# Linear attention and two MLPs on one core: two more blocks of the first MLP done as a pair by seven products of halves, with the preparation's tiles and stores arranged anew

## The chip, the cores and the metric

The kernel runs on one core of a Trainium2 chip. The metric is the device time of one execution in microseconds (us). The engines named here are TensorE (PE: matmuls; its weight loads are listed as PEld), VectorE (DVE), ScalarE (ACT), GpSimd (POOL) and SyncE (SP), which issues most of the DMA transfers. A row with a q behind the engine's name (SPq, ACTq) is that engine's instruction queue at work, for example issuing a transfer.

## The reference

All data is float32 (the weights arrive as 64-bit floats, read as pairs of 32-bit words). Three stages follow each other:

```
kv  = einsum('bhsd,bhse->bhde', k, v)              # batch 8, heads 8, seq 576, dim 64
o   = einsum('bhsd,bhde->bhse', q, kv)
x   = o / sqrt(mean(o*o, -1) + 1e-6) * g_norm      # 4608 tokens x 512
h   = x @ w_in                                     # 512 -> 2048
g   = h if h >= 1, 0 if h <= -1, else (h + 1)**2 / 4
x   = g @ w_out                                    # 2048 -> 512
h   = x @ w_in2
out = (max(h, 0)**2) @ w_out2
```

## The kernel before

**Blocks.** The 4608 tokens are nine blocks of 512 (numbered 0 to 8). Blocks 0 to 7 are the first 512 positions of the eight batch entries; block 8 collects the 64 positions that are left of each. The first MLP (L = 1) takes block after block, each in 16 steps over the 2048 inner columns. In a step `h_stage` makes 12 matmuls into one bank, ScalarE and VectorE make the activation, `g_stage` splits the result into a high and a low part, and `out_stage`, LAG = 2 steps later, adds 12 matmuls to four accumulator banks. Every product of two float32 matrices is three matmuls of high and low parts (`mm3`), each of 128 x 128 weights and 512 columns.

**Attention** of block b + 1 runs beside the steps of block b, cut into stages (`kv_stage`, `t_stage`, `o_stage`, `r_stage`) that a table of hooks puts at half steps. Attention 7 so runs beside block 6, and none runs beside blocks 7 and 8. Block 8's input, `xrd`, is stored batch entry by batch entry and loaded again.

**The second MLP** (L = 2) works on pairs of blocks, (0,1), (2,3), (4,5), (6,7), and on block 8 alone at the end. For a pair, both of its matrix products are taken as 2 x 2 halves with seven products where eight would do (`PRODUCTS`). `in_phase` goes through four groups q of seven products of two inner tiles each, reads sums and differences of halves of x (`x2_jobs`) against prepared sums and differences of halves of the weights, and makes the activation of each bank; `out_phase` goes through seven products of eight inner tiles. Each phase has 28 weight tiles with 12 matmuls for each tile. `put_out` transposes the result on VectorE and stores it, during the next pair.

**The preparation** makes those weight tiles while the first MLP runs. It has 16 units, each for two tiles of 128 rows or columns of one weight matrix of L = 2: load two raw tiles (`prep_load`), narrow them from 64 to 32 bits (`prep_narrow`, lines 227 to 230), make four sums of 256 columns (`prep_sums`, lines 294 to 298), and split four tiles (`prep_split`, line 305), storing two of them whole (`wcd`, line 308) and seven halves (`wsd`, line 315). The stores are issued by SP, as soon as the code reaches them. All its tiles share three buffers (`w1_13` to `w1_15`) with the raw loads. Those buffers are free because the last TAIL = 6 of the 16 second weight tiles of L = 1 are stored and fetched again for each block from 1 on (`load_tail`, line 254), over RING = 3 buffers.

**Order.** A planner orders the instructions of each engine by priority and by its own reckoning of when they can run, so the order written in the code is a priority and not the order of execution. At run time each engine and each queue takes its instructions in the order that the planner left.

Lines 735 (split), 758 (differences of x), 812 to 852 (`in_phase`), 862 to 923 (`out_phase`), 877 and 880 (its sums) and 665 (store of a finished block of L = 1) are spoken of below.

Of the kernel before, what the change touches and what calls it, by code (L numbers as in the profile page):

```python
# [76 lines left out]
def linear_attention_rms_two_mlps(  # L77
# [36 lines left out]
    TAIL = 6  # L114
# [4 lines left out]
    EVERY = 7  # L119
# [12 lines left out]

    x1d = [dr.tile([P, KD, TB], F32, name=f"x1d{b}") for b in range(NB)]
    xrd = dr.tile([P, KD, B, REM], F32, name="xrd")
    wtd = [dr.tile([P, 2 * TB], F32, name=f"wtd{f}") for f in range(TAIL)]
# [99 lines left out]
    def split_w(L, f, which):  # L235

        phase = int(f >= AHEAD)
        w = narrow_w(L, f, which, phase)
        dst = wi if which == 0 else wo
        t = wp.tile([P, 2, TB], F32R, tag=f"w{which}_{f}", name=f"w{L}_{which}_{f}")  # L240
        split(t, w, "w", phase)
        dst[L, f] = t
        if which == 1 and f >= NF - TAIL:
            nc.sync.dma_start(wtd[f - (NF - TAIL)], t.rearrange("p a f -> p (a f)").bitcast(F32))

# [4 lines left out]
    def load_tail(b, f):  # L250

        i = f - (NF - TAIL)
        t = wp.tile([P, 2, TB], F32R, tag=f"w1_{NF - TAIL + i % RING}", name=f"wt{b}_{f}")
        nc.sync.dma_start(t.rearrange("p a f -> p (a f)").bitcast(F32), wtd[i])
        wo[1, f] = t


    prep_tags = itertools.cycle(range(NF - RING, NF))
# [6 lines left out]
    def prep_load(which, i):  # L265
        for f in (i, i + NH):
            t = prep_tile(f"raw2_{which}_{f}", [P, 2 * TB], I32)
# [10 lines left out]
    def prep_narrow(which, i, n):  # L278
        prep[which, i, n] = narrow_w(2, i + n * NH, which, 2)

    def halves(which, i):

        w0, w1 = prep[which, i, 0], prep[which, i, 1]
        lo, hi = slice(0, H2), slice(H2, TB)
        if which == 0:
            return w0[:, lo], w0[:, hi], w1[:, lo], w1[:, hi]
        return w0[:, lo], w1[:, lo], w0[:, hi], w1[:, hi]

    def prep_sums(which, i):
        a11, a12, a21, a22 = halves(which, i)  # L290
        t = d_tile(f"s12_{which}_{i}")
        u = d_tile(f"s34_{which}_{i}")
# [6 lines left out]
        prep[which, i, 2], prep[which, i, 3] = t, u  # L299

    def prep_split(which, i, n):
        src = prep.pop((which, i, n))
        t = prep_tile(f"s2_{which}_{i}_{n}", [P, 2, TB], F32R)
        copy(engine2("s_hi"), t[:, 0, :], src)
        engine2("s_lo").tensor_tensor(t[:, 1, :], src, t[:, 0, :].bitcast(F32), ALU.subtract)
        t = t.bitcast(F32)
        if n < 2:
            nc.sync.dma_start(wcd[which, i + n * NH], t)
        made = {
            0: ((1, 2), (None, 4), (5, 6), (7, 3)),  # L310
            1: ((1, None), (2, 4), (5, 6), (7, 3)),
        }[which][n]
        for h, p in enumerate(made):
            if p:
                nc.sync.dma_start(
                    wsd[which, i // 2, p][:, i % 2], t[:, :, h * H2 : (h + 1) * H2]
                )
# [8 lines left out]
    og = {}  # L326

# [17 lines left out]
    def load_kv(b, hp):  # L345
        h0 = 2 * hp
        if b > 0:

            r = rests[hp % len(rests)]
# [56 lines left out]
    def kv_stage(b, *hps):  # L406
# [12 lines left out]
        for n, hp in enumerate(hps):  # L419
            for j in range(2):  # L420
# [8 lines left out]
                t = kvbd[hp % len(kvbd)]  # L429
# [72 lines left out]
    def o_stage(b, hp, half):  # L502
        work, parts = hl[b, hp]
        kv = kvbd[hp % len(kvbd)]
# [23 lines left out]
    def r_stage(b, hp):  # L528
# [19 lines left out]
        norm(t, y, o)  # L548
        nc.gpsimd.tensor_copy(xrem[b][:, hp, :], t[:, TB:])
        split(xs[1, b][hp], t[:, :TB], "x", b)  # L550
# [6 lines left out]
    def attention(b):  # L557
# [6 lines left out]
        def begin():  # L564
            new_x(1, b)
# [590 lines left out]
```

## Time and profile before

| | |
|---|---|
| Time, median of 3 runs | 1595.66 us (1595.51 to 1598.09) |
| Time of the profiled execution | 1596.07 us |
| Span of the profiled execution | 1594.3 us |
| PE busy | 1579.0 us (99%), 7531 matmuls |
| DVE busy | 942.4 us (59%) |
| ACT busy | 906.8 us (57%) |
| POOL busy | 111.0 us (7%) |
| Moved by DMA | 302.36 MB, mean 190 GB/s |

The span reaches from the first to the last instruction in the trace. Busy times are those of the whole span; the stages differ a lot, so the rows below are taken by stage. The end of a matmul is modelled in the profile, so that a busy PE is not PE at its peak.

### The profile page before, as it was taken

Reading aid. Unit: us, or ns where it says so; the run is one execution under the profiler, and the core shown is the slowest. Engines: PE = TensorE matmul, PEld = TensorE weight load, DVE = VectorE, ACT = ScalarE, POOL = GpSimd, SP = SyncE. Lnnn points to the kernel's source line nnn. Section 1 sums busy time; section 2 is a strip of 40 time slices with the busy share of each in tenths; the row PEclk is TensorE's granted clock in tenths of the full one; section 3 lists DMA queues with packets and bytes.
Section 4 is the critical chain, followed back from the end, with each engine's and each line's share of the span. In section 5 each row is a group of like instructions: output and inputs, shape, how many; then the busy total and the mean of one; then the engine's idle time right before and its main releaser. Section 6 shows DMA issues by size and latency. Waiting matters only on the chain.

```text
span 1594.3 us, 21133 instructions
## 1 busy us (share of the span) xinstructions
PE 1579.0 (99%) x7531; PEld 1292.5 (81%) x7533; DVE 942.4 (59%) x1558; ACT 906.8 (57%) x1649; POOL 111.0 (7%) x106
## 2 busy tenths in 40 slices
PE   9999999999999999999999999999999999999998
PEld 5788888788888888888888888888888888878886
DVE  6976756557666575643244348754974496457522
ACT  5976666666666676744344556446635663665321
POOL 0000000000000000000000121012101300330000
PEclk9999999999999999999999999999999999999999
DMA  9926656675776757522140457596768666865683
GB/s 283 281 93 164 209 163 212 178 238 185 221 218 191 235 170 226 191 71 93 53 145 27 171 190 247 189 234 208 240 193 243 218 217 202 237 220 186 189 249 104
DMA packets 306969, 302.36 MB, mean 190 GB/s; under 512 B 195504, under 2 KB 248752, under 8 KB 306864
## 3 DMA queue, kind: packets, MB, share of 16 engines
q1 hardware_dynamic: 304880, 300.22, 61.2%
q8 instruction: 60, 0.98, 0.2%
q10 hardware_dynamic: 1984, 0.79, 0.2%
q14 instruction: 45, 0.37, 0.1%
HBM read 231.74 MB, written 69.21 MB: 189 GB/s over the span
## 4 chain that ended last, share of the span: by engine, by line
PE 70%; issue 15%; DVE 9%; ACT 2%; DMA 2%; POOL 1%; SPq 0%; DVEq 0%; POOLq 0%; ACTq 0%
PE acc L197 27%; PE ph L197 26%; PE ph L790 10%; PE po L790 4%; DVE t L735 3%; DVE x L735 2%; PE po L197 1%; PE pkv L418 1%; PE pr L540 1%; POOL t L851 1%; DVE g L880 1%; DVE xr L758 1%; DMA q<-in_q_dram 0%; POOL g L852 0%; DMA wsd<-s 0%
## 5 line engine op out<-in xcount | busy, mean ns | idle before, releaser
L197 PE MATMUL ph<-x,w 128*128 128x512 f32 x1728 | 419.0, 391 | 2.4 <-ACT w L176 1.5
L197 PEld LDWEIGHTS ph<-x,w 128*128 128x128 f32 x1728 | 321.8, 188 | 70.1 <-ACT w L176 2.3
L790 PE MATMUL po<-t,ws 128*128 128x512 f32 x1344 | 307.3, 390 | 1.8 <-DVE t L735 1.8
L790 PE MATMUL ph<-x,ws 128*128 128x512 f32 x1344 | 306.5, 389 | 0.6 <-DVE e L835 0.6
L790 PEld LDWEIGHTS po<-t,ws 128*128 128x128 f32 x1344 | 251.4, 188 | 57.0 <-DVE t L735 5.0
L790 PEld LDWEIGHTS ph<-x,ws 128*128 128x128 f32 x1344 | 252.0, 188 | 54.1 <-DVE e L835 1.9
L197 PE MATMUL acc<-gs,w 128*128 128x512 f32 x1152 | 280.6, 392 | 0.0
L197 PEld LDWEIGHTS acc<-gs,w 128*128 128x128 f32 x1152 | 214.4, 188 | 44.6 <-DVE u L614 0.3
L612 ACT ACTIVATE u<-ph,halfb 128x512 f32<-128x512 f32 x144 | 99.2, 689 | 176.8 <-PE ph L197 176.6
L614 DVE SCALAR_TENSOR_TENSOR u<-u,ph 128x512 f32<-128x512 f32 x144 | 98.4, 683 | 166.3 <-ACT u L183 165.9
L735 DVE TENSOR_TENSOR t<-g,t 128x512 fp32r<-128x512 f32 x192 | 134.7, 708 | 74.2 <-ACT t L176 71.8
L176 ACT CAST t<-g 128x512 fp32r<-128x512 f32 x192 | 116.4, 621 | 71.4 <-DVE t L735 50.8
L189 DVE TENSOR_TENSOR gs<-u,gs 128x512 fp32r<-128x512 f32 x160 | 110.4, 690 | 63.2 <-ACT gs L176 62.0
L176 ACT CAST gs<-u 128x512 fp32r<-128x512 f32 x160 | 99.4, 621 | 75.2 <-DVE u L614 58.0
L197 PE MATMUL acc<-gs,wt 128*128 128x512 f32 x576 | 139.4, 391 | 0.0
L197 PEld LDWEIGHTS acc<-gs,wt 128*128 128x128 f32 x576 | 106.8, 188 | 21.6
L843 DVE TENSOR_TENSOR h<-ph,e 128x512 f32<-128x512 f32 x96 | 66.1, 691 | 55.9 <-PE ph L790 50.2
L844 ACT ACTIVATE h<-h 128x512 f32<-128x512 f32 x96 | 60.5, 630 | 60.0 <-DVE h L843 56.0
L183 ACT ACTIVATE u<-u 128x512 f32<-128x512 f32 x144 | 91.1, 632 | 2.2
L851 POOL TENSOR_TENSOR t<-g 128x512 f32<-128x512 f32 x32 | 43.1, 1347 | 633.7 <-ACT g L845 353.2
L845 ACT ACTIVATE g<-h 128x512 f32<-128x512 f32 x128 | 80.9, 632 | 3.6
L835 DVE TENSOR_TENSOR e<-ph,e 128x512 f32<-128x512 f32 x64 | 43.4, 688 | 44.3 <-PE ph L790 43.2
(116 smaller groups left out, 1415.0 us busy)
## 6 DMA issues: line engine op xcount, KB each, us to landing
ws<-wsd SPq DMA_DIRECT2D x224, 512.0 KB, 3.5
wsd<-s SPq DMA_DIRECT2D x112, 256.0 KB, 3.8
wt<-wtd SPq DMA_DIRECT2D x48, 512.0 KB, 4.4
raw<-in_moe_w_in_dram SPq DMA_DIRECT2D x32, 512.0 KB, 5.9
raw<-in_moe_w_out_dram SPq DMA_DIRECT2D x32, 512.0 KB, 5.7
wcd<-s SPq DMA_DIRECT2D x32, 512.0 KB, 3.6
ws<-wcd SPq DMA_DIRECT2D x32, 512.0 KB, 4.3
x1d<-ev SPq DMA_DIRECT2D x36, 256.0 KB, 3.0
```

The source lines that it names most:

```text
L176: return e.copy(dst, src)
L183: e.activation(dst, src, AF.Square)
L189: lo = engine(op + "_lo", phase).tensor_tensor(t[:, 1, :], src, t[:, 0, :].bitcast(F32), ALU.subtract)
L197: nc.tensor.matmul(dst, wt(a), xt(c), start=first and n == 0, stop=last and n == 2)
L612: nc.scalar.activation(u, ps, AF.Relu, bias=halfb, scale=0.5)
L614: nc.vector.scalar_tensor_tensor(u, u, 1.0, ps, op0=ALU.min, op1=ALU.max)
L735: engine2(op + "_lo").tensor_tensor(t[:, 1, :], src, t[:, 0, :].bitcast(F32), ALU.subtract)
L790: nc.tensor.matmul(ps, wt(a), xt(c), start=first and n == 0 and i == 0, stop=last and n == len(lhs) - 1 and i == 2, skip_group_check=True,)
L843: nc.vector.tensor_tensor(h, bank, add, ALU.add)
L844: nc.scalar.activation(h, h, AF.Relu)
L845: nc.scalar.activation(g, h, AF.Square)
L851: engine2("t_sum").tensor_tensor(t1[k], b, a, ALU.subtract)
```

## The change

Blocks 7 and 8 leave the plain loop of the first MLP. They are taken as a pair (1, 7), third in a list of five pairs, by the same two phases that the pairs of the second MLP use, with the first MLP's activation and with all 16 differences of the activations (`t_sum`) on VectorE for that pair. Attention 7 stores its result (`xpd`, `xrd`) and the pair loads it through `x2_jobs`. The result of the pair is stored to `x1d` without a transpose.

For this the weights of L = 1 must be there as sums and differences of halves too. Each unit of the preparation goes on after its four tiles of L = 2: it adds the high and low parts of two tiles of L = 1 (`prep_join`), makes their four sums, and splits and stores two more tiles. `keep_first` stores those halves of the L = 1 tiles that are themselves used. Nine tail tiles are fetched for each block, where it was six. The raw tiles have two buffers of their own, the split tiles four. All weight tiles are laid out as [128, half, high or low, 256], and each matrix pair has one store `wsd[L, w, a]` of eight slots, from which both the halves and whole tiles are read; `wcd` and `wtd` go.

Stores of split tiles and of finished blocks no longer go out on SP at once: `owe` notes them with a delay of two half steps (one for finished blocks), and `pay`, called once in each half step, issues them on ScalarE's queue. The hooks are numbered by half steps; `o_stage` and `r_stage` come one half step later, the first x load of a next pair comes six products earlier.

```diff
-    TAIL = 6
+    TAIL = 9
...
+    PLAIN = B - 1
+    PAIRS = [(2, 0), (2, 2), (1, PLAIN), (2, 4), (2, 6)]
+    LAST_B = B - 1
...
     wsd = {
-        (w, a, p): dr.tile([P, 2, 2, H2], F32, name=f"wsd{w}_{a}_{p}")
+        (L, w, a): dr.tile([P, 8, 2, 2, H2], F32, name=f"wsd{L}_{w}_{a}")
+        for L in (1, 2)
         for w in range(2)
         for a in range(NQ)
-        for p in PRODUCTS
     }
-    wcd = {(w, f): dr.tile([P, 2, TB], F32, name=f"wcd{w}_{f}") for w in range(2) for f in range(NF)}
...
+    MADE = {
+        0: (1, 2, None, 4, 5, 6, 7, 3),
+        1: (1, None, 2, 4, 5, 6, 7, 3),
+    }
+    def keep_halves(L, which, i, n, t, now=False):
+        made = MADE[which][2 * n : 2 * n + 2]
+        hs = slice(0, 2)
+        if L == 1 and None in made and not (which == 1 and i + n * NH >= NF - TAIL):
+            hs = slice(1, 2) if made[0] is None else slice(0, 1)
+        dst = wsd[L, which, i // 2][:, 2 * n + hs.start : 2 * n + hs.stop, i % 2]
+        if now:
+            nc.sync.dma_start(dst, t[:, hs])
+        else:
+            owe(2, dst, t[:, hs])
+    owed = []
+    tick = [0]
+    def owe(wait, dst, src):
+        owed.append((tick[0] + wait, dst, src))
+    def pay(every=False):
+        for job in list(owed):
+            due, dst, src = job
+            if every or due <= tick[0]:
+                nc.scalar.dma_start(dst, src)
+                owed.remove(job)
+        tick[0] += 1
+    def split_halves(t, src, hi, lo):
+        src = src.rearrange("p (h f) -> p h f", h=2)
+        copy(hi, t[:, :, 0, :], src)
+        lo.tensor_tensor(t[:, :, 1, :], src, t[:, :, 0, :].bitcast(F32), ALU.subtract)
...
+    raw_tags = itertools.cycle((NF - TAIL + RING, NF - TAIL + RING + 1))
+    prep_tags = itertools.cycle(range(NF - TAIL + RING + 2, NF))
...
+    def prep_join(L, which, i):
+        for n in range(2):
+            f = i + n * NH
+            t = prep.get((L, which, i, n))
+            if t is not None:
+                d, w = t[:, :, 0, :], t
+            else:
+                w = (wi[L, f] if which == 0 else wo[L, f]).bitcast(F32)
+                d = d_tile(f"j_{which}_{f}").rearrange("p (h f) -> p h f", h=2)
+            nc.vector.tensor_tensor(d, w[:, :, 0, :], w[:, :, 1, :], ALU.add)
+            prep[L, which, i, n] = d
...
+    def prep_split(L, which, i, n):
+        src = prep.pop((L, which, i, n))
+        t = prep_tile(f"s{L}_{which}_{i}_{n}", [P, 2, 2, H2], F32R)
+        split_halves(t, src, engine2("s_hi"), engine2("s_lo"))
+        keep_halves(L, which, i, n, t.bitcast(F32))
+    def keep_first(which, f):
+        t = wi[1, f] if which == 0 else wo[1, f]
+        keep_halves(1, which, f % NH, f // NH, t.bitcast(F32), now=True)
...
+        xt = st.tile([P, TB], F32, tag="st", name=f"xt_{hp}")
+        nc.vector.scalar_tensor_tensor(t, t, -3.0, y, op0=ALU.add, op1=ALU.mult)
+        nc.vector.tensor_tensor(xt, o[:, :TB], t[:, :TB], ALU.mult)
+        nc.vector.tensor_tensor(xrem[b][:, hp, :], o[:, TB:], t[:, TB:], ALU.mult)
+        x_kept[hp] = xt
+    x_kept = {}
+    def keep_x(b, hp):
+        nc.sync.dma_start(xpd[:, hp, :], x_kept.pop(hp))
+        nc.sync.dma_start(xrd[:, hp, b, :], xrem[b][:, hp, :])
...
+                (s + 3, o_stage, b, hp, 0),
+                (s + 4, o_stage, b, hp, 1),
...
+            slots.append((s + 6, r_stage, b, hp))
+            if b == LAST_B:
+                slots.append((s + 8, keep_x, b, hp))
...
-            nc.sync.dma_start(x1d[b][:, c, :], t)
+            owe(1, x1d[b][:, c, :], t)
...
+    def x_source(n, b, ch, t):
+        L, b0 = PAIRS[n]
+        if L == 2:
+            return t, x1d[b0 + b][:, ch, :]
+        if b == 0:
+            return t, xpd[:, ch, :]
+        return t.rearrange("p (b s) -> p b s", b=B), xrd[:, ch, :, :]
...
-                        h = tmp.tile([P, TB], F32, f"h{n}_{p}_{k}")
-                        if p == 2:
-                            nc.scalar.activation(h, bank, AF.Relu)
-                        else:
+                        h = bank
+                        if p != 2:
+                            h = tmp.tile([P, TB], F32, f"h{n}_{p}_{k}")
                             add = e[i, {5: 7, 4: 1, 3: 6}[p]]
                             nc.vector.tensor_tensor(h, bank, add, ALU.add)
-                            nc.scalar.activation(h, h, AF.Relu)
-                        nc.scalar.activation(g, h, AF.Square)
+                        if PAIRS[n][0] == 1:
+                            nc.scalar.activation(g, h, AF.Relu, bias=halfb, scale=0.5)
+                            nc.scalar.activation(g, g, AF.Square)
+                            nc.vector.scalar_tensor_tensor(g, g, 1.0, h, op0=ALU.min, op1=ALU.max)
+                        else:
+                            u = tmp.tile([P, TB], F32, f"u{n}_{p}_{k}") if p == 2 else h
+                            nc.scalar.activation(u, h, AF.Relu)
+                            nc.scalar.activation(g, u, AF.Square)
                 yield
             for i in range(2):
                 k = 2 * q + i
                 a, b, d = g2[k][0][:, 0, :], g2[k][0][:, 1, :], g2[k][1][:, 1, :]
                 t1[k] = t1_ring.tile([P, TB], F32, f"t1_{n}_{k}")
-                engine2("t_sum").tensor_tensor(t1[k], b, a, ALU.subtract)
-                engine2("t_sum").tensor_tensor(b, d, b, ALU.subtract)
+                for dst, x, y in ((t1[k], b, a), (b, d, b)):
+                    e = nc.vector if PAIRS[n][0] == 1 else engine2("t_sum")
+                    e.tensor_tensor(dst, x, y, ALU.subtract)
...
+        if L == 1:
+            for m in range(2):
+                nc.sync.dma_start(x1d[b][:, 2 * hm + m, :], result[n](hm, m, hn))
+            return
...
+    kept = [(w, f) for f in range(NF) for w in range(2) if w == 0 or f < NF - TAIL]
+    for j, (w, f) in enumerate(kept):
+        hook(2 * (NF + 2) + 3 * j, keep_first, w, f)
...
     for j in range(2 * NH):
         which, i = j % 2, j // 2
-        s0 = NF + 2 + (7 * j * (7 * NF - 8)) // (7 * 2 * NH)
-        for d, half, f, a in (
-            (0, 0, prep_load, ()),
-            (1, 0, prep_narrow, (0,)),
-            (2, 0, prep_narrow, (1,)),
-            (3, 0, prep_sums, ()),
-            (3, 1, prep_split, (0,)),
-            (4, 0, prep_split, (1,)),
-            (4, 1, prep_split, (2,)),
-            (5, 0, prep_split, (3,)),
+        s0 = 2 * NF + 4 + (j * 164) // 16
+        for d, L, f, a in (
+            (-6, 2, prep_load, ()),
+            (2, 2, prep_narrow, (0,)),
+            (3, 2, prep_narrow, (1,)),
+            (4, 2, prep_sums, ()),
+            (4, 2, prep_split, (0,)),
+            (5, 2, prep_split, (1,)),
+            (6, 2, prep_split, (2,)),
+            (7, 2, prep_split, (3,)),
+            (7, 1, prep_load, ()),
+            (9, 1, prep_join, ()),
+            (10, 1, prep_sums, ()),
+            (10, 1, prep_split, (2,)),
+            (11, 1, prep_split, (3,)),
         ):
-            hook(0, s0 + d, half, f, which, i, *a)
-    last = (NB - 1) * NF
+            hook(s0 + d, f, L, which, i, *a)
...
+    last = 2 * (PLAIN - 1) * NF
     first_x = x2_jobs(0, Ring(*[(st, "st")] * 7))
     when = [0, 1, 2, 3, 4, 5, 6, 7, 5, 8, 9, 10, 11, 12, 13, 14]
     for t, f in zip(when, first_x):
-        hook(0, last + t, 1, f)
-    for i in range(7):
-        hook(0, last - 3 + i if i < 3 else last + i, 1, load_w2)
+        hook(last + 2 * t + 1, f)
+    for i, t in enumerate((7, 9, 11, 13, 15, 21, 23)):
+        hook(last + t, load_w2)
...
+            pay(True)
...
-        at = range(8, 8 + 2 * len(jobs), 2)
+        at = (2, *range(10, 8 + 2 * len(jobs), 2))
```

## Rows read from the trace of the kernel before

**Rows 1.** Windows: busy us by engine, PE's clock, DMA share, GB/s
```profile
45.00:141.00 96.00, 94.56 (x502) 74.24 (x501) 75.69 (x138) 74.57 (x147) 2.56 (x4) 1.00 0.58 177
141.00:237.80 96.80, 96.80 (x510) 80.04 (x509) 62.42 (x112) 64.51 (x127) 1.80 (x4) 1.00 0.63 187
...
335.70:432.70 97.00, 97.00 (x512) 80.87 (x511) 59.13 (x104) 62.82 (x123) 1.36 (x4) 1.00 0.70 214
...
717.10:804.10 87.00, 87.00 (x385) 72.03 (x384) 27.61 (x42) 34.76 (x56) 0.00 (x0) 1.00 0.22 73
...
1038.00:1115.00 77.00, 76.79 (x339) 63.29 (x338) 36.15 (x54) 42.98 (x72) 17.90 (x12) 1.00 0.77 220
1115.00:1192.00 77.00, 76.77 (x338) 62.84 (x337) 64.08 (x98) 42.69 (x75) 6.30 (x4) 1.00 0.67 218
```

**Rows 2.** Waits: engine, line, releaser: us in total, times, longest us
```profile
DVE u L614 <- ACT u L183: 165.9, 73, 4.3
...
PE po L790 <- DVE t L735: 1.8, 4, 1.1
```

**Rows 3.** Timeline of SP: stores of finished blocks (start us, us)
```profile
716.92 2.25 SPq L665 DMA_DIRECT2D x1d<-ev  x4
...
803.96 1.15 SPq L665 DMA_DIRECT2D x1d<-ev  x2
...
891.00 2.25 SPq L665 DMA_DIRECT2D x1d<-ev  x4
```

**Rows 4.** The chain that ended last: the same place in two pairs
```profile
1086.42 28.88 PE ph L790 x126
...
1240.07 28.87 PE ph L790 x126
```

**Rows 5.** Instruction groups: busy us, mean ns of one; idle before, releaser
```profile
L614 DVE SCALAR_TENSOR_TENSOR u<-u,ph 128x512 f32<-128x512 f32 x144 | 98.4, 683 | 166.3 <-ACT u L183 165.9
...
L843 DVE TENSOR_TENSOR h<-ph,e 128x512 f32<-128x512 f32 x96 | 66.1, 691 | 55.9 <-PE ph L790 50.2 <-ACT h L844 5.7
...
L230 DVE SCALAR_TENSOR_TENSOR d<-raw,d 128x512 int32<-128x512 int32 x64 | 43.7, 686 | 4.9 <-ACT raw L227 3.6
L835 DVE TENSOR_TENSOR e<-ph,e 128x512 f32<-128x512 f32 x64 | 43.4, 688 | 44.3 <-PE ph L790 43.2
...
L227 ACT ACTIVATE raw<-raw 128x512 f32<-128x512 f32 x64 | 42.7, 679 | 17.7 <-DMA raw<-in_moe_w_in_dram 9.7 <-DMA raw<-in_moe_w_out_dram 4.4 <-DMA wt<-wtd 3.6
...
L229 DVE TENSOR_SCALAR d<-raw 128x512 int32<-128x512 int32 x64 | 26.6, 419 | 19.8 <-DMA raw<-in_moe_w_in_dram 13.3 <-DMA raw<-in_moe_w_out_dram 6.4
...
L305 DVE TENSOR_TENSOR s<-s,s 128x512 fp32r<-128x512 f32 x32 | 21.9, 684 | 2.5 <-ACT s L176 2.2
...
L176 ACT CAST s<-s 128x512 fp32r<-128x512 f32 x32 | 19.9, 623 | 5.6 <-DVE s L297 3.4 <-DMA wsd<-s 2.2
...
L294 DVE TENSOR_TENSOR s<-d 128x256 f32<-128x256 f32 x8 | 3.4, 419 | 0.1
```

**Rows 6.** Windows: two stretches of the first block, same columns
```profile
65.00:75.00 10.00, 10.00 (x44) 7.79 (x43) 9.73 (x19) 9.94 (x21) 0.00 (x0) 1.00 1.01 307
95.00:105.00 10.00, 10.00 (x61) 8.07 (x60) 10.00 (x20) 9.90 (x20) 0.24 (x1) 1.00 0.69 249
```

**Rows 7.** Timelines of SP's and ACT's queues: issues (start us, us)
```profile
159.15 1.25 SPq L315 DMA_DIRECT2D wsd<-s  x2
...
0.76 0.74 ACTq L400 DMA_DIRECT2D kvr<-in_k_dram  x1
```

**Rows 8.** Waits of SP's queue: us in total, times, longest
```profile
SPq L308 <- DVE s L305: 51.7, 10, 19.7
```

**Rows 9.** The tile of the tail weights, its loads
```profile
DMA to landing us min/median/max: 3.1/4.4/10.1
```

**Rows 10.** Timeline of 1086 to 1115 us (start us, us)
```profile
1086.42 28.86 PE L790 MATMUL ph<-x,ws 128*128 128x512 f32 x126 [0.21 <-DVE e L835]
...
1099.70 0.69 DVE L877 TENSOR_TENSOR g<-g,t 128x512 f32<-128x512 f32 x1 [1.37 <-POOL t L851]
```

More of the change, by code (lines that the diff above doesn't have):

```diff
@@ L239, in split_w, with kept_whole @@
         dst = wi if which == 0 else wo
-        t = wp.tile([P, 2, TB], F32R, tag=f"w{which}_{f}", name=f"w{L}_{which}_{f}")
-        split(t, w, "w", phase)
+        t = wp.tile([P, 2, 2, H2], F32R, tag=f"w{which}_{f}", name=f"w{L}_{which}_{f}")
+        split_halves(t, w, engine("w_hi", phase), engine("w_lo", phase))
         dst[L, f] = t
         if which == 1 and f >= NF - TAIL:
-            nc.sync.dma_start(wtd[f - (NF - TAIL)], t.rearrange("p a f -> p (a f)").bitcast(F32))
+            keep_halves(L, which, f % NH, f // NH, t.bitcast(F32), now=True)
+    def kept_whole(L, which, f):
+        return wsd[L, which, f % NH // 2][:, f // NH * 2 : f // NH * 2 + 2, f % 2]
     def split_later(*a):
@@ L276, in prep_load, with prep_narrow, halves, prep_sums @@
             w_raw[2, f, which] = t.rearrange("p (f two) -> p f two", two=2)
[L278 to L284, printed above, removed]
-        if which == 0:
[L286 to L292, printed above, removed]
+    def prep_join(L, which, i):
+        for n in range(2):
+            f = i + n * NH
+            t = prep.get((L, which, i, n))
[6 more added lines that the diff above has]
+            prep[L, which, i, n] = d
+    def prep_narrow(L, which, i, n):
+        prep[L, which, i, n] = narrow_w(2, i + n * NH, which, 2)
+    def halves(L, which, i):
+        w0, w1 = prep[L, which, i, 0], prep[L, which, i, 1]
+        if L == 2:
+            w0, w1 = (w.rearrange("p (h f) -> p h f", h=2) for w in (w0, w1))
+        if which == 0:
+            return w0[:, 0, :], w0[:, 1, :], w1[:, 0, :], w1[:, 1, :]
+        return w0[:, 0, :], w1[:, 0, :], w0[:, 1, :], w1[:, 1, :]
+    def prep_sums(L, which, i):
+        a11, a12, a21, a22 = halves(L, which, i)
+        t = d_tile(f"s12_{L}_{which}_{i}")
+        u = d_tile(f"s34_{L}_{which}_{i}")
         s1, s2, s3, s4 = t[:, :H2], t[:, H2:], u[:, :H2], u[:, H2:]
@@ L555, in new_x, with begin, attention_first @@
         ]
-    def attention(b):
+    def begin(b):
+        if b < LAST_B:
+            new_x(1, b)
+        xrem[b] = ap2.tile([P, KD, REM], F32, tag="xrem", name=f"xrem_{b}")
+    def attention_first():
         slots = {}
@@ L719, in load_w2 @@
             return
-        whole = len(key) == 2
-        t = w_ring.tile([P, 2, TB] if whole else [P, 2, 2, H2], F32R, "ws" + "_".join(map(str, key)))
-        nc.sync.dma_start(t.bitcast(F32), (wcd if whole else wsd)[key])
+        name = "ws" + "_".join(map(str, key))
+        if len(key) == 4:
+            t = w_ring.tile([P, 2, 2, H2], F32R, name)
+            L, which, a, p = key
+            nc.sync.dma_start(t.bitcast(F32), wsd[L, which, a][:, MADE[which].index(p)])
+        else:
+            which, f = key
+            t = w_ring.tile([P, 2, 2, H2], F32R, name)
+            nc.sync.dma_start(t.bitcast(F32), kept_whole(2, which, f))
         w_loaded.append((key, t))
@@ L950, in put_out @@
                 nc.sync.dma_start(rows[a], src)
[L952 removed]
+    blocks = [(1, b) for b in range(PLAIN)]
     hooks = {}
[L955 to L994 removed]
@@ new lines, in hook @@
+    def hook(s, f, *a):
+        hooks.setdefault((s // 2, s % 2), []).append((f, a))
+    jobs = [(0, store_xrem, 0)]
+    for b in range(1, B):
+        jobs += attention(b, 2 * NF * (b - 1), 7, range(NP))
+    for job in sorted(jobs, key=lambda j: j[0]):
+        hook(*job)
+    for i in range(NF):
+        later = split_later if i < 2 else split_w
+        for w, ahead, at in ((0, 7, 6), (1, 6, 3)):
+            if i + ahead < NF:
+                hook(2 * i + w, load_w, 1, i + ahead, w)
+            if i + at < NF:
+                hook(2 * i + w, later, 1, i + at, w)
@@ L1052, in linear_attention_rms_two_mlps @@
     nc.gpsimd.memset(kvw, 0.0)
-    first = attention(0)
+    first = attention_first()
     for s, n in WARMS:
```

180 lines of the change are left out of this document (68 added, 112 removed).

## The prediction

> **What bounds the kernel now.** First the busy time by stage [rows 1]. TensorE is busy for the whole of every window after the start, at granted clock 1.00, which is its level of 2.4 GHz, and the number of matmuls in a window follows the length of the window: 385 records in the 87.00 us of a first-layer block beside which no attention runs, 339 and 338 in the two halves of a pair of the second layer. VectorE is busy for 28 to 79% of these windows, ScalarE for 40 to 78%. Then the waits: the longest that TensorE has against another engine in the pairs sums to 1.8 us in four times [rows 2]. Then the moments at which the blocks end. The stores of the evicted block follow each other by 803.96 - 716.92 = 87.04 and 891.00 - 803.96 = 87.04 us [rows 3]; a block is 16 steps of 12 + 12 matmuls, 384, so one takes 226.7 ns. A pair of the second layer has 672 matmuls (28 weight tiles of 12 in each half) and comes round after 1240.07 - 1086.42 = 153.65 us [rows 4], 228.6 ns each. So time goes by the count of matmuls, at one price, in stages with VectorE nearly idle and in stages with VectorE at 83%. The profiled run took 1596.07 us for a span of 1594.3, so 1.8 lie outside it; the median of the runs shown is 1595.66, 0.4 less. I sum against 1596.07 and take 0.4 off.
>
> **The change, part by part.**
>
> *The pair in place of blocks 7 and 8.* Two blocks of 87.04 us go: block 7's attention is already done during block 6, and stays there. One more round of the pair loop comes: 153.65 us, with its two transitions, since the period is taken from round to round. Net 174.08 - 153.65 = -20.4 us. By the count it is 96 matmuls at 226.7 ns, -21.8; the 1.3 us between are the pair's own small gaps. I take -20.4.
>
> *The activation inside the new pair.* Per bank of the first product stage it keeps the two ScalarE steps and adds one VectorE step that reads the sum a second time (32 in all; like line 614, 683 ns: 21.9 us), and it moves 16 differences from GpSimd to VectorE (684 ns by line 305: 10.9 us) [rows 5]. VectorE had 36.15 us of work in that half [rows 1]; it gets 36.15 + 21.9 + 10.9 = 69 of 77 us, 90%. The second half already runs with 64.08 of 77, and TensorE's longest wait there, the 1.8 us of [rows 2], is that stage's. Below: nothing. Above: the rival in order, below. I take 0.5 us. The following pair loses the 8 transposes of `put_out`, off the path: nothing.
>
> *The preparation.* A unit (there are 16) had on VectorE 2 x (419 + 686) + 4 x 419 + 4 x 684 ns = 6.6 us, on ScalarE 2 x 679 + 4 x 623 = 3.85 us [rows 5]. Now it also joins two first-layer tiles, makes their four sums, and splits two more tiles: + 2 x 684 + 4 x 419 + 2 x 684 = 4.4 us on VectorE (11.0), + 1.25 on ScalarE (5.1). The units were spread over 104 steps, 2.46 a block; now over 164 half steps, 3.12 a block. Block 3 (the window from 335.7 [rows 1]) then goes on VectorE from 59.1 to 59.1 - 16.3 + 34.5 = 77 us of 97, 80%, and on ScalarE from 62.8 to 62.8 - 9.5 + 15.9 = 69 us. The cover is shown by the first block, with 75.69 and 74.57 us of 96, 79 and 78%, and TensorE busy for 94.56 of them; and stretches of 10 us in which both engines stand at 9.7 to 10.0 have TensorE at 10.00 as well [rows 6]. LAG holds two steps between activation and second product, so short crowding is swallowed. I take 0.5 us for the seven blocks, bounds 0 and what the rivals give.
>
> *Stores from ScalarE's queue.* Six stores a unit and four of each block's result are issued from ScalarE: 6 x 3.12 + 4 = 23 a block. An issue of such a store takes SP 1.25/2 = 0.63 us, and one on ScalarE's own queue took 0.74 [rows 7]. So ScalarE gets 14 to 17 us more, 83 to 86 of 97. A store waiting at the head would hold the activations behind it, and the matmuls behind those; being due two half steps (6 us) after the split was issued, it should find its tile written. ScalarE would pass TensorE's 97 us only if an issue cost (97 - 69)/23 = 1.2 us. Below: nothing; above: nothing up to 1.2. I take nothing. SP loses the waits that it had at these stores (51.7 us in ten at line 308 alone [rows 8]), so the loads behind them (tails, raw tiles, q, k, v) leave earlier; as nothing on TensorE waits for them now, that gains nothing.
>
> *The rings of their own.* Raw tiles get two tiles and split tiles four, where both shared three; nine tail tiles a block are fetched over three buffers, not six. A tail load still leaves when the product three before it ends and is due two steps later, about 13 us; it lands after 4.4 us in the middle and 10.1 at most [rows 9]. Nothing, unless the DMA engines fill up.
>
> *What the DMA engines get.* A unit moved 2 raw tiles, 2 whole and 7 half stores, 3.9 MB; now 2 raw, 4 + 2 whole stores and 9/16 of a load, 4.5 MB: 9.7 to 14.0 MB a block. Three tails more are 1.6 MB. The kept first-layer tiles are 8.1 MB over 67 half steps, 3.9 MB a block in blocks 1 to 3. That is 9.8 MB a block more there, 5.9 after. The window at 717.1 moved 73 GB/s at a share of 0.22 [rows 1], 6.35 MB, so 1 MB costs 87 x 0.22 / 6.35 = 3.0 us of all sixteen. On 0.63 to 0.70 of a block (the windows from 141 and 335.7) come 0.30, making 0.93 to 1.0 in blocks 1 to 3, and 0.81 to 0.88 after. I take 1 us; the bounds are in the rivals. The Trainium skill, page "DMA: Bandwidth & Descriptors", section "Issuing engines are not separate DMA queues", says that transfers issued by several engines run on the same sixteen and interleave, so that a second issuer saves issue time alone. No row before shows stores from ScalarE's queue beside loads from SP's. By that rule the moved stores relieve the engines of nothing and the 1 us stands; were ScalarE's queue apart, it would be 0.
>
> *The rest.* First x loads of a pair go out at product 2, not 8, in a stage without a wait for them: nothing. Attention's o and r stages move one half step later; o's and r's matmuls waited for nothing that counts: nothing. The first pair's x tiles and attention 7 now share the seven `st` buffers in block 6; a load that waits there for a buffer holds SP, and could hold TensorE at `kv_stage` by about a landing, 4 us [rows 9]. I take nothing, bound 4.
>
> **Sum.** 1596.07 - 20.4 + 0.5 + 0.5 + 1 = 1577.7, as a median 1577.3; I say 1577.5.
>
> **The rivals.**
>
> *The DMA engines fill up (0.18).* For: 0.93 to 1.0 by the sum above, in blocks 1 to 3. Against: stores now go out in runs of 2 KB for 1 KB, and loads have 13 us and more of lead. Were the demand 5% over, the backlog would be 2.1 x 97 x 0.05 = 10 us, which TensorE would spend waiting for tails or k and v: about 1587; it begins to cost above 1.0. The case runs from 1581 to 1592. By the rule named above this case keeps its chance; without it the chance would be near nothing.
>
> *VectorE takes the new pair's steps in the written order (0.07, slower).* Place: the first half of the new pair. In the code each bank's third step follows its add at once. If VectorE stood still between them while ScalarE does two steps (1.32 us), a bank would cost 0.69 + 1.32 + 0.68 + 0.05 = 2.75 us, against 1.37 that TensorE takes for it. Four rounds of 6 such banks, 2 without the add (2.0 each), 4 adds and 4 differences are 104 us, with the 8.5 of transposes and preparation 112 for 77: +35, so about 1612. It decides from 20 us of such standing on. For it: VectorE stood 165.9 us in 73 times for just this pair of steps in the plain blocks [rows 2], where it had nothing else. Against: the planner doesn't keep the written order; a difference of the out phase (line 877) ran at 1099.70 while the in phase's matmuls went on to 1115 [rows 10].
>
> *The saving is given back (0.05, within 0.2%).* TensorE's full look hides other limits, and the saved 20 us return as small waits in the seven heavy blocks, 3 us in each: about 1596. For: ScalarE and VectorE both over 80% there. Against: the first block, where both stand at 79% without it [rows 1], and the 10 us stretches without any slack [rows 6].
>
> *More than summed (0.04):* the count's 21.8 and some of the pairs' waits, under 1573.5.
>
> **From this to the numbers.** The forecast, gain kept but for 0 to 4 us of waits, has 0.66 and 1573.5 to 1581. Up to 1588 lie some 0.13 of the first rival, so 1573.5 to 1588 holds 0.79. A difference under 0.2% (3.2 us; the runs shown spread over 2.6) can't be told from none. Faster by more: 0.66 + 0.18 + 0.04 = 0.88; the same 0.05; slower 0.07.
>
> **What the profile will show.** If right: blocks 7 and 8 gone from the plain matmuls, 96 matmuls fewer, a fifth round of some 154 us between the second and third old pair; VectorE near 69 us in its first half and near 80% in blocks 1 to 6, ScalarE a few points above; DMA share over 0.9 in blocks 1 to 3; TensorE's waits together a few us. It is wrong if the new first half is well over 80 us long, if a plain block with attention takes more than about 98 us (waits for tails, k and v, or activations), or if ScalarE's queue stands at its stores.

## The result, and the profile after

The changed kernel takes 1577.82 us in the median of four runs (1576.82 to 1580.16), the kernel before 1595.61: a ratio of 0.9889, 95% interval [0.9876, 0.9901]. The forecast was 1577.5 us, with a range of 1573.5 to 1588. The profiled execution has a span of 1575.3 us where it was 1594.3.

Where the 19.0 us of the span come from is read off the moments at which the phases of the pairs begin. This is the timeline of TensorE after the change (start us, us, what; a row joins matmuls of one group until a gap):

```profile
709.64 2.88 PE L883 MATMUL ph<-x,ws 128*128 128x512 f32 x12
...
791.24 26.52 PE L883 MATMUL po<-t,ws 128*128 128x512 f32 x115
817.97 50.43 PE L883 MATMUL po<-t,ws 128*128 128x512 f32 x221 [0.22 <-DVE t L819]
...
944.95 26.47 PE L883 MATMUL po<-t,ws 128*128 128x512 f32 x115
...
1021.90 76.32 PE L883 MATMUL ph<-x,ws 128*128 128x512 f32 x336
1098.06 76.32 PE L883 MATMUL po<-t,ws 128*128 128x512 f32 x336
1174.22 76.32 PE L883 MATMUL ph<-x,ws 128*128 128x512 f32 x336
```

The first pair begins at 709.64; before it began at 881.24. That is 171.6 us earlier where two blocks of 87.04 are 174.08: the first layer lost 2.5 us. From there to the end it takes 865.66 us where it took 713.06: the fifth pair costs 152.6 and not 153.65. Together 174.08 - 2.5 - 152.6 = 19.0. The new pair is the one from 1021.90 to 1174.22, 152.32 us for 672 matmuls, 226.7 ns each: its two phases have no gap at all, where the first pair's second phase breaks after 115 matmuls. There the row names a wait of 0.22 us, but the 116th matmul starts 26.73 us after the first and not 115 x 0.2267 = 26.07, so the break costs 0.66.

The windows after, columns as in [rows 1]: blocks 1 to 3, then the two phases of the new pair.

```profile
141.00:237.00 96.00, 95.77 (x505) 79.33 (x504) 74.82 (x142) 66.93 (x133) 2.08 (x4) 1.00 0.92 287
237.00:333.00 96.00, 96.00 (x507) 79.94 (x506) 74.29 (x139) 66.69 (x133) 3.02 (x4) 1.00 0.95 293
333.00:429.00 96.00, 96.00 (x506) 79.91 (x505) 75.37 (x139) 67.18 (x135) 3.68 (x4) 1.00 0.81 248
...
1021.90:1098.00 76.10, 76.10 (x337) 63.06 (x336) 60.45 (x96) 46.62 (x74) 0.00 (x0) 1.00 0.78 220
1098.00:1174.20 76.20, 76.20 (x337) 63.11 (x337) 62.13 (x101) 41.95 (x73) 0.00 (x0) 1.00 0.77 242
```

VectorE went to 78% and the DMA share to 0.92 to 0.95 in blocks 1 and 2, and TensorE stays full. The first layer has one wait that it did not have before, at the end of block 5. The waits after (engine, line, releaser: us in total, times, longest), and the timeline of that place:

```profile
ACT ev L739 <- DMA x1d<-ev: 4.3, 1, 4.3
...
PE acc L237 <- ACT ev L739: 2.9, 1, 2.9
```

```profile
622.57 0.34 ACTq L176 DMA_DIRECT2D x1d<-ev  x1
...
624.38 0.34 ACTq L176 DMA_DIRECT2D x1d<-ev  x1
...
625.29 2.21 PE L237 MATMUL acc<-gs,w 128*128 128x512 f32 x9
...
629.81 0.58 ACT L739 COPY ev<-acc 128x512 f32<-128x512 f32 x1 [4.29 <-DMA x1d<-ev]
...
630.45 1.65 PE L237 MATMUL acc<-gs,w 128*128 128x512 f32 x3 [2.94 <-ACT ev L739]
...
631.89 3.59 PE L237 MATMUL ph<-x,w 128*128 128x512 f32 x12
```

The fourth copy of the evicted block finds no free buffer in the ring of seven and takes that of the first copy, which must first land in DRAM: its store was issued at 622.57 and the copy starts at 629.81, 7.2 us later. TensorE, which needs the fourth accumulator bank, stands behind it.

With the slower matmuls behind it (last section) this wait costs 4.4 us, more than the 2.5 that the layer lost in all. Elsewhere the layer is shorter: before, TensorE had stood 1.65 us for the transposed q in block 2, and after it does not. What took that wait away was not tested. Before:

```profile
299.85 0.40 PE L197 MATMUL po<-qT,kvbd 128*128 128x288 f32 x1 [1.26 <-ACT qT L176]
300.64 0.54 PE L197 MATMUL po<-qT,kvbd 128*128 128x288 f32 x2 [0.39 <-DVE qT L499]
```

### The profile page after: what moved, and what is told of

The parts are those of the page before. It is cut to its first block, busy times and chain, and to the rows that moved or that the text cites. A ratio compares the mean times of both kernels' runs of the same rounds, so it can differ in the third digit from the quotient of the medians.

```text
span 1575.3 us, 21493 instructions
## 1 busy us (share of the span) xinstructions
PE 1557.6 (99%) x7435; PEld 1275.3 (81%) x7437; DVE 1068.6 (68%) x1806; ACT 939.0 (60%) x1719; POOL 116.9 (7%) x102
## 5 line engine op out<-in xcount | busy, mean ns | idle before, releaser
L883 PE MATMUL po<-t,ws 128*128 128x512 f32 x1680 | 383.7, 390 | 2.4 <-DVE t L819 2.4
L883 PE MATMUL ph<-x,ws 128*128 128x512 f32 x1680 | 382.6, 389 | 0.4 <-DVE e L928 0.4
L883 PEld LDWEIGHTS po<-t,ws 128*128 128x128 f32 x1680 | 314.6, 188 | 70.7 <-DVE t L819 5.6
L883 PEld LDWEIGHTS ph<-x,ws 128*128 128x128 f32 x1680 | 315.2, 188 | 66.7 <-DVE e L928 1.3
L237 PE MATMUL ph<-x,w 128*128 128x512 f32 x1344 | 329.8, 393 | 2.5 <-ACT w L216 1.6
L237 PEld LDWEIGHTS ph<-x,w 128*128 128x128 f32 x1344 | 249.8, 188 | 56.4 <-ACT w L216 2.8
L819 DVE TENSOR_TENSOR t<-g,t 128x512 fp32r<-128x512 f32 x240 | 167.6, 704 | 79.7 <-ACT t L216 76.8
L237 PE MATMUL acc<-gs,w 128*128 128x512 f32 x696 | 174.4, 395 | 2.9 <-ACT ev L739 2.9
L237 PEld LDWEIGHTS acc<-gs,w 128*128 128x128 f32 x696 | 129.3, 188 | 29.6 <-ACT ev L739 3.4
L216 ACT CAST x<-xr 128x512 fp32r<-128x512 f32 x74 | 45.9, 621 | 47.8 <-DVE xr L851 34.0
```

Source lines behind the costliest of these rows:

```text
L216: return e.copy(dst, src)
L237: nc.tensor.matmul(dst, wt(a), xt(c), start=first and n == 0, stop=last and n == 2)
L819: engine2(op + "_lo").tensor_tensor(t[:, 1, :], src, t[:, 0, :].bitcast(F32), ALU.subtract)
L883: nc.tensor.matmul(ps, wt(a), xt(c), start=first and n == 0 and i == 0, stop=last and n == len(lhs) - 1 and i == 2, skip_group_check=True,)
```

## The experiments

All times are medians; the interval belongs to the ratio to the kernel before. The kernel before had 1595.81, 1596.44 and 1596.29 us in the three groups of runs (1 to 4, 5 to 8, 9 to 12), so a difference of some 0.6 us between runs of different groups says nothing.

**1. First x loads two steps later.** (On the changed kernel.)

```diff
-    when = [0, 1, 2, 3, 4, 5, 6, 7, 5, 8, 9, 10, 11, 12, 13, 14]
+    when = [2, 3, 4, 5, 6, 7, 8, 9, 7, 10, 11, 12, 13, 14, 15, 15]
```

> The first x loads of the first pair leave two steps later, so that they no longer hold buffers of the shared ring of seven while block 5 is evicted. Theory (the eviction's last copy waits for a buffer, TensorE waits 2.9 us behind it and runs at its lower clock for some 2 us after): the wait of ScalarE for the store of the finished block is gone, TensorE's wait of 2.9 us too, time 1577.8 - 3 to 4.5 = 1573.5 to 1575. Rival (the lost 2.5 us are the heavier load of VectorE and of the DMA engines in blocks 1 to 6, and the wait is only where it shows): the wait moves to another tile, time within 1 us of 1577.8.

1573.55 us (1573.03 to 1574.04), 0.9861 [0.9847, 0.9874]. Both waits are gone from the trace (ScalarE still stands 2.4 us beside these stores, but nothing on TensorE waits for it), and its first pair begins at 705.97, 3.7 us earlier. The theory holds: one wait made the loss, not the heavier load.

**2. Finished blocks stored by SP at once.**

```diff
-            owe(1, x1d[b][:, c, :], t)
+            nc.sync.dma_start(x1d[b][:, c, :], t)
```

> The stores of finished blocks go out on SP at once, as before the change; everything else as changed. If the half step of delay and ScalarE's queue make the eviction wait, the wait at block 5 shrinks from 4.3 us to under 2 and the time falls by 2 to 3 us to about 1575. If the ring of buffers itself is short at that place, the last copy still waits for a landing (about 5 us at a DMA share of 0.84): 1577 to 1578, or more where SP stands at a load in front of the store.

1581.62 us, 0.9909 [0.9896, 0.9923]: above the 1577 to 1578 of the second theory, which allowed for more where SP stands. ScalarE's wait for the store is gone with this edit too (these stores land 2.6 to 4.5 us after their issue, where the one waited for had taken 7.2); but the first pair begins 6.8 us later (716.40), with a new wait in its trace:

```profile
PE po L237 <- ACT qT L216: 4.5, 4, 1.7
```

SP now stands at these stores (10.6 us in nine times for VectorE's copies alone). Before the longest of TensorE's new waits, at 557.68, VectorE had stood 4.37 us at the load of a first-layer tile (`wf`), and it transposed q only after that, at 556.15:

```profile
551.39 0.69 DVE L340 TENSOR_TENSOR wf<-wf 128x512 f32<-128x512 f32 x1 [4.37 <-DMA wf<-wsd]
```

That the stores made this load late is likely but not shown. So the wait at the ring goes in two ways, by stores from SP (here) and by x loads that leave the ring free (run 1), and only the second gains time; this run alone does not tell whether the delayed store or the short ring is at fault.

**3. The differences on VectorE in all pairs**, and **4. both edits**.

```diff
-    "t_sum": "P",
+    "t_sum": "D",
```

> The differences of the activations go to VectorE in all five pairs, not in the new one alone. The new pair takes 152.3 us with no gap, the others 153.1 to 153.7. If GpSimd's 1.3 and 1.8 us for such a step make the small gaps at the start of the second products, each old pair comes to about 152.4 to 152.8: 3 to 4 us less in all, 1574 to 1575. If the gaps come from the transposes of the stored result on VectorE or from the pair's own order, nothing: 1577 to 1578.5.

> Both of the two edits above (first x loads two steps later, differences on VectorE in all pairs). If each cause is its own, the gains add: 1577.8 - 3.5 - 3.5 = about 1571, between 1569.5 and 1572.5. If one of them is none, about 1574.5.

1571.78 us, 0.9849 [0.9835, 0.9862], and with both 1567.76 us, 0.9824 [0.9811, 0.9838]. The gains, 6.0 and 4.3, add up to 10.3; both edits together gain 10.1. TensorE's timeline in the third run, the second phases of the first two pairs:

```profile
791.84 76.32 PE L883 MATMUL po<-t,ws 128*128 128x512 f32 x336
...
944.16 76.32 PE L883 MATMUL po<-t,ws 128*128 128x512 f32 x336
```

Every pair now has the 152.32 us of the new one. GpSimd's differences made the breaks. The gain is above the 3 to 4 us expected, since the changed kernel's old pairs had lost 0.8, 1.3, 0.8 and 2.6 us, 5.6 in all, and the expectation had left out how long the last one was.

GpSimd's step is not only longer, it also makes VectorE's steps beside it longer. This is the changed kernel where the first pair's second phase begins, VectorE and GpSimd:

```profile
792.25 1.29 POOL L951 TENSOR_TENSOR t<-g 128x512 f32<-128x512 f32 x1 [13.33 <-DMA ws<-wsd]
793.46 0.69 DVE L819 TENSOR_TENSOR t<-g,t 128x512 fp32r<-128x512 f32 x1 [1.25 <-ACT t L216]
793.62 1.68 POOL L951 TENSOR_TENSOR g<-g,g 128x512 f32<-128x512 f32 x1
794.24 1.61 DVE L976 TENSOR_TENSOR g<-g,t 128x512 f32<-128x512 f32 x1
795.26 1.74 POOL L951 TENSOR_TENSOR t<-g 128x512 f32<-128x512 f32 x1
795.77 1.78 DVE L819 TENSOR_TENSOR x<-xr,x 128x512 fp32r<-128x512 f32 x1
797.08 1.63 POOL L951 TENSOR_TENSOR g<-g,g 128x512 f32<-128x512 f32 x1
797.48 1.78 DVE L819 TENSOR_TENSOR t<-g,t 128x512 fp32r<-128x512 f32 x1
```

Three steps of VectorE take 1.61 to 1.78 us where 0.69 is usual. Three such steps stand at the start of the second phase of all four old pairs, before the change and after, and run 3, in which GpSimd has no differences, has none. How much of the 5.6 us is GpSimd's own step and how much VectorE's was not parted.

**5. Attention's o and r stages half a step earlier**, as before the change. (This one and the next three on top of edit 1, so against 1573.55.)

```diff
-                (s + 3, o_stage, b, hp, 0),
-                (s + 4, o_stage, b, hp, 1),
+                (s + 2, o_stage, b, hp, 0),
+                (s + 3, o_stage, b, hp, 1),
...
-                slots.append((s + 6, begin, b))
-            slots.append((s + 6, r_stage, b, hp))
+                slots.append((s + 5, begin, b))
+            slots.append((s + 5, r_stage, b, hp))
```

> On top of the first x loads two steps later (1573.55 us): attention's o and r stages back to where they stood before the change, one half step earlier. If TensorE has nothing to wait for there either way, as was predicted, 1573 to 1574.5. Rival: with VectorE and ScalarE at 75% and 70% of blocks 1 to 5 the earlier place makes TensorE wait for the transposed q or the squares (four attention heads in seven blocks, some 0.3 us each): 1577 to 1582.

1577.12 us (1576.82 to 1579.10), 0.9882 [0.9866, 0.9899]: 3.6 us slower by the medians, though the intervals overlap; 0.6 of it is the difference that the kernel before shows between the two groups. The edit also moves `begin`, which makes the tiles of attention's result. The first pair begins 3.0 us later (708.96), and TensorE waits 1.8 us in two times for VectorE's `u`, where it did not wait. The later place is worth about 3 us. That the heavier load makes it so is not shown: 1.7 of the 1.8 us are one wait at 106.97, in block 0, before the preparation begins.

**6. Stores of split tiles by SP at once.**

```diff
         if now:
             nc.sync.dma_start(dst, t[:, hs])
         else:
-            owe(2, dst, t[:, hs])
+            nc.sync.dma_start(dst, t[:, hs])
```

> On top of the first x loads two steps later (1573.55 us): all stores of split tiles go out on SP at once, as before the change, and ScalarE keeps only the stores of finished blocks. If the moved stores gain nothing, as was predicted, 1573 to 1574.5. Rival: SP stands at each store until its tile is split (51.7 us in ten at one line before the change), and with 4.5 MB a unit the tails, k, v and q behind it come late: TensorE waits some us in each of blocks 1 to 6, 1580 to 1600.

1617.28 us, 1.0129 [1.0114, 1.0145]: 43.7 us slower, more than the rival said, and slower than before the change. SP's two longest waits at its stores, its queue around the longer one with VectorE's step that ends it, then four windows of 5 us (columns as above), then TensorE's timeline there:

```profile
SPq L160 <- DVE s L181: 99.4, 32, 16.7
SPq L160 <- DVE d L266: 40.2, 4, 20.7
```

```profile
277.68 3.08 SPq L431 DMA_DIRECT2D q<-in_q_dram  x2
300.49 0.68 DVE L181 TENSOR_TENSOR s<-s,s 128x512 fp32r<-128x512 f32 x1
301.20 1.32 SPq L160 DMA_DIRECT2D wsd<-s  x2
```

```profile
290.00:295.00 5.00, 4.19 (x19) 2.79 (x18) 2.83 (x4) 5.00 (x13) 0.00 (x0) 1.00 0.00 0
295.00:300.00 5.00, 5.00 (x23) 4.11 (x24) 3.72 (x8) 4.06 (x8) 0.00 (x0) 1.00 0.00 0
300.00:305.00 5.00, 3.32 (x15) 2.43 (x13) 5.00 (x12) 2.94 (x6) 1.56 (x1) 1.00 0.60 214
305.00:310.00 5.00, 0.41 (x1) 0.41 (x2) 5.00 (x10) 2.02 (x4) 4.03 (x1) 0.80 0.92 228
```

```profile
309.59 2.07 PE L234 MATMUL ph<-x,w 128*128 128x512 f32 x4 [6.27 <-DVE u L703]
```

From 280.76 to 301.20 SP issues nothing: it stands at a store whose tile VectorE splits only at 300.49 (the row of the wait names line 266, a step that ran beside the end of it). For ten microseconds nothing moves (share 0.00), then VectorE is full with work that came due together, and TensorE stands 6.27 us at an activation queued behind it.

**7. Each split tile of the second MLP stored twice.**

```diff
             owe(2, dst, t[:, hs])
+            if L == 2:
+                owe(2, spare[which, i, n], t)
```

> On top of the first x loads two steps later (1573.55 us): each split tile of the second MLP is stored a second time, to a place that nobody reads, by ScalarE's queue: 64 stores more, 33.6 MB, 6.5 MB a block. The share of the DMA engines in the two windows from 141 us stands at 0.93 and 0.96. Theory that a share of 1.0 is the point from which it costs: demand becomes 1.1 to 1.15, a backlog of 10 to 15 us a block in blocks 1 to 3, less what the leads of 13 us hide: 1585 to 1605. Rival (the leads and the lighter blocks after 3 take the backlog): under 1576, with the share at 1.0 and longer landings.

1644.36 us, 1.0301 [1.0285, 1.0316], 71 us more, and not by the way expected: the DMA share stays at 0.79 to 0.93. VectorE's longest wait, and SP's at the load in front of it:

```profile
DVE wf L349 <- DMA wf<-wsd: 40.8, 6, 10.6
SPq L324 <- DMA spare<-s: 15.5, 7, 4.4
```

A tile is held until both stores have landed, the next load into its buffer (line 324) waits on SP for the second store, `spare`, and VectorE stands at that load. So this run raised two things, the traffic and the time that a buffer is held, and another run had to part them.

**8. The new pair's differences on GpSimd.**

```diff
-                    e = nc.vector if PAIRS[n][0] == 1 else engine2("t_sum")
+                    e = engine2("t_sum")
```

> On top of the first x loads two steps later (1573.55 us): the new pair's 16 differences on GpSimd, as in the other pairs. The new pair takes 152.3 us without a gap. If GpSimd's differences make the gaps in the other pairs, the new pair gets them too, 153.0 to 153.7: 1574.3 to 1575. If the pairs' gaps come from the transposes, of which the new pair has as many as the others, no change: 1573.5.

1581.69 us, 0.9908 [0.9893, 0.9923], 8.1 us slower. TensorE's timeline: the new pair lasts from 1019.13 to 1176.51, 157.4 us, 5.1 more, with breaks up to 1.91 us. The theory of GpSimd's differences has the direction right, but its 153.0 to 153.7 us are far exceeded.

```profile
1067.44 30.22 PE L883 MATMUL ph<-x,ws 128*128 128x512 f32 x132 [1.91 <-DVE e L928]
```

In this pair GpSimd's step also meets VectorE's third step of the activation: in each of the four groups one such step takes 1.77 to 1.78 us, where none takes over 0.69 in the changed kernel. From 1176.51 to the end it is 2.3 us slower too, and the first layer 0.9; why the rest moved with this edit stays open.

**9. Copies that hold no tile.**

```diff
+    def extra(which, i, n):
+        f = i + n % 2 * NH
+        src = w_src[2][1][f * P : (f + 1) * P, :]
+        nc.sync.dma_start(spare[which, i, n], src)
...
         keep_halves(L, which, i, n, t.bitcast(F32))
+        if L == 2:
+            extra(which, i, n)
```

> On top of the first x loads two steps later (1573.55 us): beside each of the 64 splits of the second MLP's weights, SP issues a copy of 512 KB from one place in DRAM to another that holds no tile and waits for none: 33.6 MB, 6.5 MB a block. The run that stored each split tile twice went to 1644 us with the DMA share at 0.88 to 0.93 only, and VectorE standing at a load of a split-ring tile (40.8 us in six). If it was the tiles that stayed occupied, these copies cost little: under 1580, with the share at 0.95 to 1.0. If it was the load on the DMA engines, they cost as much: 1610 to 1650.

1596.89 us, 1.0005 [0.9996, 1.0015]: between the two theories, 23.3 us for 33.6 MB (on top of edit 1, as run 12 is). The same bytes cost 71 us when they held tiles, so some two thirds of that would be the tiles. The two runs differ in more, though: run 7's stores go out on ScalarE's queue, and run 9's copies on SP's, reading as many bytes from DRAM as they write. Two windows, and the landing of the tail loads:

```profile
333.00:429.00 96.00, 93.61 (x460) 77.28 (x459) 71.14 (x131) 62.96 (x126) 1.30 (x4) 1.00 0.98 324
...
524.50:622.00 97.50, 91.77 (x484) 75.48 (x483) 72.61 (x135) 62.96 (x129) 1.11 (x3) 1.00 0.97 314
```

```profile
DMA to landing us min/median/max: 3.6/6.4/11.6
```

Tails land after 6.4 us where the changed kernel has 5.1, and TensorE's largest single waits (2.9 us for an activation, 2.7 for the transposed q, 2.4 behind ScalarE's narrowing of a raw tile) are spread over several tiles. The load does cost, and at mean shares of 0.95 to 0.99 already, though not evenly: TensorE stood 2.4 us of the window of block 3 (share 0.98, above), 5.7 of the last one shown (0.97), and not at all between them, from 429.0 to 524.5 (share 0.99).

**10. The first x load at product 8 again** (on top of both edits, against 1567.76).

```diff
-        at = (2, *range(10, 8 + 2 * len(jobs), 2))
+        at = range(8, 8 + 2 * len(jobs), 2)
```

> On top of the first x loads two steps later and the differences on VectorE everywhere (1567.76 us): the first x load of each next pair at product 8 again, as before the change. If the early load is worth nothing, as was predicted, 1567 to 1568.5. Rival: the load lands at product 10's split too late and holds ScalarE (1.4 us at most in the kernel before) and TensorE behind it: 1569 to 1572.

1568.35 us, 0.9826 [0.9813, 0.9839]. Nothing that can be told.

**11. The kernel before with its differences on VectorE.** The edit is that of the third run.

> The kernel before with its differences of the activations on VectorE instead of GpSimd and nothing else. Four pairs of 153.65 us become about 152.3 to 152.6, and the 1.1 us wait at the second product of the last pair goes: 4 x 1.1 to 1.4 plus about 1, 5 to 6.5 us less than 1596, 1589.5 to 1591. If the new pair's evenness is a matter of its place in the order (no transposes after it), 1595 to 1596.

1590.51 us, 0.9963 [0.9951, 0.9975]: 5.8 us less without anything of the change. Its pairs have phases of 336 matmuls in 76.32 us as well. So the evenness of the new pair is owed to the engine of its differences, not to its place.

**12. The delay kept, but on SP.**

```diff
-                nc.scalar.dma_start(dst, src)
+                nc.sync.dma_start(dst, src)
```

> On top of the first x loads two steps later (1573.55 us): all delayed stores keep their delay of two half steps (one for finished blocks) but are issued by SP. Stores at once on SP gave 1617 us, delayed on ScalarE 1573.55. If the delay is what counts (no queue stands at a store for its tile), 1573 to 1577. If ScalarE's queue is what counts (SP has too much to issue in order), nearer to 1617: 1590 to 1617.

1625.49 us, 1.0184 [1.0171, 1.0197]; here the stores of finished blocks are SP's as well, which had cost 3.8 us in run 2. SP's longest wait at a store there:

```profile
SPq L176 <- DVE s L184: 133.7, 29, 19.2
```

The delay alone saves nothing. What helps is that loads no longer stand in a queue behind stores that wait for VectorE. That it is the time of issuing instead is unlikely: in run 9 SP issued 64 transfers more that wait for no tile, and with all the load that they bring these cost 23.3 us, against 43.7 and 51.9 for the 96 stores and more of runs 6 and 12. Why SP reaches these stores early in spite of the delay was not traced; the planner's order is the place to look.

## Why the prediction was right, and where it was not

**The bound and the main term** were right. Time goes by the count of matmuls: the saved 96 are worth 21.8 us at 226.7 ns, and the span shows 174.08 - 152.6 = 21.5 for the exchange of two blocks for a pair. (The shares of VectorE in the prediction's first paragraph, "28 to 79%", are misread: its rows give 32 to 83%. Nothing in the sum hangs on it.) The forecast term of -20.4 was 1 us short, since it took the new pair at 153.65 us with the gaps of the old ones. Those gaps belong to GpSimd's differences (runs 3, 8, 11), which the new pair does not have. Having them on VectorE was part of a term of +0.5 us; it was a gain (run 8, without it, takes 8.1 us more).

**The activation in the new pair** was put at 69 us of VectorE in 77; it is 60.45 of 76.1 for 96 instructions, and costs TensorE nothing. The rival in the written order fell: it needed 20 us of standing between adds and third steps, and VectorE waited 7.3 us in nine times at the third steps of that half. Its timeline shows adds and third steps taken in turn.

```profile
1055.53 0.69 DVE L939 SCALAR_TENSOR_TENSOR g<-g,h 128x512 f32<-128x512 f32 x1
1056.13 0.68 DVE L935 TENSOR_TENSOR h<-ph,e 128x512 f32<-128x512 f32 x1
...
1056.89 0.69 DVE L939 SCALAR_TENSOR_TENSOR g<-g,h 128x512 f32<-128x512 f32 x1
1057.49 0.68 DVE L935 TENSOR_TENSOR h<-ph,e 128x512 f32<-128x512 f32 x1
```

**The preparation** was put at 77 us of VectorE and a DMA share of 0.93 to 1.0 in blocks 1 to 3; it is 74 to 75 us, and 0.92, 0.95 and 0.81. TensorE swallowed it, as forecast.

**The shared ring** was the one wait that did come. I named the seven `st` buffers, bounded them at 4 us and took nothing. The price was near (4.3 us, run 1), the value taken wrong, and the place another than `kv_stage`: it was the eviction. The 2 us of waits in the sum stood for the new pair, the preparation and the DMA engines, and no wait of TensorE over 0.3 us was found in their places. That the sum is within 0.5 us of the time is luck: this wait of 4.4 us, taken at nothing, stands in their place, and the first layer's other gains and the 1.1 us of the pair make up the rest.

**Stores from ScalarE's queue** is the step whose reasoning failed. "As nothing on TensorE waits for them now, that gains nothing" was read from the trace before, where SP's standing (51.7 us at one line) cost TensorE nothing. Under the new load it does: with the stores back on SP the kernel takes 43.7 us more (run 6), and the change is a loss against the kernel before. The forecast held because it took the cover for granted and not because it knew it. The same holds at a smaller size for attention's half step, which was put at nothing and is worth about 3 us in run 5.

**The DMA engines** have less room than forecast. The point from which load costs was put above a share of 1.0; run 9 costs 23 us with mean shares of 0.90 to 0.99 in blocks 1 to 5. Tails land 1.3 us later there than in the changed kernel; whether such landings make TensorE's waits, or short backlogs that a mean share hides, was not told apart. From 141 to 333 the packets of SP's queue took 64.4% of the sixteen engines and those of ScalarE's 28.9%, which add up to the share of 0.92 to 0.95. The rule weighed in the prediction (the Trainium skill, "DMA: Bandwidth & Descriptors", "Issuing engines are not separate DMA queues"), that both run on the same sixteen, agrees with this. Its remark that a second issuer saves issue time alone falls short here: runs 6 and 12 take 44 and 52 us more with these stores on SP, and their rows show SP standing at stores, not issuing.

## What to carry to other kernels

In these runs SP, issuing both loads and stores, stood at each store until its tile was written, and the loads behind it stood as well; before adding work to such a kernel, part the two, and count how long SP stands even where it costs nothing yet. A ring of buffers that gets a new user should be followed through one whole turn, with the user that comes last and the landing of its store as the price. When phases of the same count of matmuls differ by a microsecond, look at which engine makes the inputs of the slower one: 64 steps of 1.3 to 1.7 us on GpSimd were worth 6 us in all when VectorE took them at 0.7, though VectorE was the busier engine; GpSimd's steps had slowed VectorE's own beside them as well. The version with both edits takes 1567.76 us, 0.9824 of the kernel before.

## What the runs showed of the hardware

**This wait cost more than its length.** After TensorE's stand of 2.94 us the granted clock was at its lower level, 1.2 GHz, for about 3 us. Windows of the changed kernel there, columns as above:

```profile
630.40:631.40 1.00, 0.95 (x2) 0.83 (x3) 0.00 (x0) 1.00 (x3) 0.00 (x0) 0.50 0.28 115
631.40:632.40 1.00, 1.00 (x4) 0.74 (x3) 0.57 (x1) 1.00 (x3) 0.00 (x0) 0.50 0.49 190
...
633.40:634.40 1.00, 1.00 (x5) 0.81 (x5) 0.49 (x1) 0.00 (x0) 0.00 (x0) 1.00 0.81 102
```

The 15 matmuls from 630.45 to 635.32 took 4.87 us where 3.40 are usual. With the stand that is 4.4 us, and taking the wait away gave 4.3.

**Durations of VectorE overlap.** The mean of one step is 0.68 to 0.69 us, but steps that wait for nothing start 0.60 us apart (1055.53 and 1056.13 above), so a sum of durations overstates a VectorE without pauses by some 13 to 15%. Of the new pair's first half, 69 us forecast and 60.45 found, this is one part: its 96 steps of 0.68 to 0.69 us sum to 66 us. The rest is that 96 steps fell into it and not the 102 of the forecast (54 before, 32 and 16 more).

**Issues of transfers on ScalarE** took 0.34 us in the rows above and 0.37 in the median of the 96 stores of split tiles, not the 0.63 to 0.74 that the rows before had suggested.

**VectorE and GpSimd slow each other.** In the rows of run 3, VectorE's steps of 0.69 us took up to 1.78 beside GpSimd's differences, and GpSimd's `t` took 1.74 us beside them, where it takes 1.29 alone (at 792.25, there). Not every step of VectorE beside GpSimd is slowed: of some 60 in the changed kernel that overlap one, 12 took over 0.9 us.
